# A reordered static schedule for an attention and multiplicative-FFN kernel, meant to issue the loads of the prologue earlier

## The chip, the cores and the metric

The kernel runs on one core of one Trainium2 chip. The metric is the device time of one execution in microseconds (us), best seen as the median of several; the executions of one kernel, six at most in one run, lay within 0.3 to 0.7 % of each other.

The engines are named as in the profile: PE (matmuls), PEld (its weight loads), DVE (vector), ACT (scalar), POOL (GpSimd) and SP, which here mostly issues DMAs.

## The reference, cut to what matters

```python
# 8 batches, 8 heads, 576 positions, 64 wide; float32
q_s = softmax(q, axis=-1);  k_s = softmax(k, axis=2)           # over features, over positions
kv  = einsum('bhsd,bhse->bhde', k_s, v)
x   = einsum('bhsd,bhde->bhse', q_s, kv)  -> (4608, 512)        # tokens x (heads * 64)
a, b = x @ w1, x @ w2                                          # 512 -> 1024, twice
out  = ((a * b) @ w3) @ w_out                                  # 1024 -> 1024 -> 512
```

## The kernel before: the parts that the change and the argument touch

The kernel multiplies W3 by W_out once (`W3O`), runs the attention batch by batch, and feeds groups of tokens to the FFN. Its 1477 steps are made first, as objects; nothing is emitted. Three literal tables then decide everything that a scheduler decides: `ORDER`, the order in which the steps are emitted (and so the order within each engine and each DMA queue, as every engine works in order), `SLOTS`, which buffer of its pool each step's buffer is, and `ENGS`, the engine of each step that can run on more than one.

```python
class Steps:
    ...
    def run(self, order, slots, engs):
        for b, s in zip(self.bufs, slots):
            b.tile = self.pools[b.pool][s]
        for n in order:
            if isinstance(n, tuple):
                self.fill(self.pools[n[0]][n[1]], n[2])      # matmuls on a blank tile
            elif self.tasks[n].alts:
                self.tasks[n].emit(engs[n])
            else:
                self.tasks[n].emit()
...
    tiles("st", 9, [P, 2 * RK * D], F32)      # staging: all loads land here
    tiles("osb", 4, [P, C], F32)              # output rows before their store
    tiles("ps", 8, [P, 512], F32, psum)       # the eight PSUM banks
```

A load takes one of the nine staging buffers. It is issued on the SP queue, behind all loads and SP stores emitted before it, and can't be issued before the step that last read its staging buffer is done. So the order of loads, and the buffers they reuse, decide whether the DMA queue ever runs empty.

```python
    def load(key, nbytes, rate, desc, view, src):
        b = buf("st")
        def emit():
            nc.sync.dma_start(out=view(b.tile), in_=src)
        ld[key] = (add("SP", ("ld",) + key, emit, [], [b], ...), b, view)
```

In the attention of one batch each of q, k and v comes in two pieces (four heads each). For q: exponential on ACT, sum and reciprocal on DVE, then a scaling (`qn`) on DVE or POOL, transposes on PE for batches 0 to 3 and a transposing DMA after, evictions of those (`qv`), and the x matmuls, whose PSUM banks are evicted (`xc`) by DVE or ACT into `xt`. For v: one cast to fp16 (`vc`), on POOL in most cases.

```python
            def norm(e, eq=eq, ds=ds):
                {"POOL": nc.gpsimd, "DVE": nc.vector}[e].tensor_tensor(
                    out=eq.tile, in0=eq.tile, op=ALU.mult, in1=...)   # eq * 1/sum
            ...
            t3 = add("POOL", ("qn", b, i), norm, [tr_], [eq, ds], dict(POOL="nt", DVE="tts"), n=1152)
...
                tx = add("PE", ("x", b, i, r0), xm, tn[i] + t5, [kv2, qsT, xt_buf[g]] + px, ...)
```

The FFN's first group is plain; the later ones use a Strassen-type scheme with seven products, whose sums are taken while PSUM is evicted (names `e1` to `e3`, `k1`, `k2`, `k4`; `k3` and `k5` multiply the two factors of the FFN), with helper sums of x (`tt`), of the weights (`wc`) and, for one group's second product, of `W3O` (`sT`) and of the hidden rows (`sS`). Every PE step needs free PSUM banks, so a late eviction on DVE or ACT stops PE.

The softmax here doesn't subtract the row's maximum and nothing guards it: scores larger than these inputs give would overflow.

## Time and profile before

| | before |
|---|---|
| time, median of 6 runs beside the new kernel | 230.99 us (230.84 to 231.96) |
| span of the profiled run (its time 231.96, the slowest of the six) | 230.0 us |
| span of a second profile of the same kernel (time 230.74) | 228.8 us |
| PE busy | 219.9 us, 96 % |
| DVE, ACT, POOL busy | 182.8, 142.0, 102.2 us |

How to read it: PE is the bound, and all that can be won lies in the few us in which it stands. The busy share doesn't show those well. "Perfetto Trace Analysis" of the Trainium skill says at its head, of a kernel's distance from the roofline, that matmul busy time is a bad metric, because matmuls are pipelined; here too the busy time of PE comes out the same for two kernels 1.5 us apart, as the result shows. So I read the timeline and the chain of waits, and for comparing two orders I use a **lag**: the time at which a PE step starts, minus the work of all PE steps before it (each matmul counted at the distance between starts that the trace shows for its shape). A stretch where the lag stays flat is run at PE's own pace; each rise is a wait.

### The profile page before, as it was taken

The page shows a single profiled execution, that of the slowest core. Times are in us where ns is not written, and L with a number is a line of the kernel's source. Part 1 is how long each engine was busy: PE and PEld are TensorE (multiplying, and loading weights), DVE is VectorE, ACT ScalarE, POOL GpSimd, SP SyncE. Part 2 cuts the span into 40 slices and gives each one's busy share as a digit, 9 for nine tenths or more (in the row PEclk, how much of TensorE's full clock was granted, in tenths as well). Part 3 has the DMA queues.
Part 4 walks back from the last instruction along what each step waited for, and adds up shares of the span by engine and source line. Part 5 has one row for each costly group of instructions (what it writes and reads, how often), then busy time and mean ns, then how long its engine had stood idle before and what let it go on. Part 6 is the DMA issues. An engine that isn't in the chain of part 4 may idle for free.

```text
span 230.0 us, 5284 instructions
## 1 busy us (share of the span) xinstructions
PE 219.9 (96%) x1971; PEld 124.6 (54%) x1971; DVE 182.8 (79%) x392; ACT 142.0 (62%) x289; POOL 102.2 (44%) x84
## 2 busy tenths in 40 slices
PE   7699999999999999999999999999999899999992
PEld 3354548866676564444445656543444367766640
DVE  0332865789999998999967989999999999889820
ACT  2236875768768998777527658766799474354021
POOL 4313745584064990197940268800299920310000
PEclk9999999999999999999999999999999999999999
DMA  6999997981998679919786976669885502124556
GB/s 222 390 404 391 392 388 268 379 330 13 353 371 333 158 242 278 372 50 337 180 211 171 278 278 171 128 111 297 274 204 165 75 0 48 24 68 92 116 131 165
DMA packets 32888, 50.92 MB, mean 221 GB/s; under 512 B 11744, under 2 KB 12000, under 8 KB 32864
## 3 DMA queue, kind: packets, MB, share of 16 engines
q1 hardware_dynamic: 31504, 48.57, 66.5%
q10 hardware_dynamic: 1360, 2.03, 3.8%
q8 instruction: 15, 0.25, 0.5%
q14 instruction: 9, 0.07, 0.1%
HBM read 38.80 MB, written 9.44 MB: 210 GB/s over the span
## 4 chain that ended last, share of the span: by engine, by line
PE 72%; DVE 10%; DMA 8%; ACT 3%; issue 2%; POOL 2%; SPq 2%; DVEq 0%; ACTq 0%
PE ps L648 31%; PE ps L739 17%; PE ps L591 7%; PE ps L377 6%; PE ps L836 5%; DMA st<-in_moe_w_dram 3%; DMA out_dram<-osb 2%; DMA qsT<-eq 2%; DVE cc L672 2%; PE ps L511 2%; PE ps L556 2%; DVE tt L626 2%; DVE ds L459 1%; POOL eq L469 1%; PE ps L485 1%
## 5 line engine op out<-in xcount | busy, mean ns | idle before, releaser
L672 DVE TENSOR_TENSOR cc<-ps,uu 128x512 f16<-128x512 f32 (+3 forms) x120 | 65.2, 570 | 2.8 <-PE ps L648 0.7
L344 ACT COPY uu<-ps 128x512 f32<-128x512 f32 (+3 forms) x107 | 50.4, 501 | 25.9 <-PE ps L648 14.9
L699 POOL TENSOR_TENSOR ab<-cc,cc 128x512 f16<-128x512 f16 (+3 forms) x25 | 23.1, 927 | 70.2 <-DVE cc L672 59.4
L739 PE MATMUL ps<-W3O,ab 128*128 128x512 f16 (+1 forms) x224 | 53.4, 372 | 0.0
L648 PE MATMUL ps<-tt,wc 128*128 128x512 f16 (+3 forms) x240 | 52.1, 334 | 0.3
L648 PEld LDWEIGHTS <-wc 128*128 128x128 f16 x320 | 31.0, 98 | 25.6 <-DVE tt L626 1.4
L648 PE MATMUL ps<-xt,w 128*128 128x512 f16 (+3 forms) x160 | 36.6, 334 | 0.5 <-ACT osb L725 0.5
L648 PEld LDWEIGHTS <-w 128*128 128x128 f16 x240 | 22.6, 98 | 18.1 <-issue 1.8
L739 PEld LDWEIGHTS <-ab 128*128 128x128 f16 x224 | 21.4, 98 | 20.1 <-issue 0.6
L469 POOL TENSOR_TENSOR eq<-eq,ds 128x1152 f16<-128x1152 f16 x13 | 27.9, 2152 | 6.6 <-DVE ds L466 3.3
L725 ACT ACTIVATE osb<-ps 128x512 f32<-128x512 f32 (+1 forms) x24 | 13.3, 566 | 22.5 <-PE ps L739 19.9
L459 DVE TENSOR_REDUCE ds<-eq 128x9 f32<-128x576 f16 x32 | 23.4, 740 | 4.0 <-ACT eq L455 4.0
L672 DVE TENSOR_TENSOR ab<-ps,cc 128x512 f16<-128x512 f32 (+3 forms) x40 | 22.4, 567 | 1.8 <-PE ps L648 0.6
L455 ACT ACTIVATE eq<-st 128x576 f16<-128x576 f32 x32 | 21.5, 686 | 1.1 <-DMA st<-in_q_dram 1.0
L434 ACT ACTIVATE ek<-st 128x576 f16<-128x576 f32 x32 | 21.0, 688 | 1.6 <-DMA st<-in_k_dram 1.3
L344 ACT CAST xt<-ps 128x320 f16<-128x320 f32 (+7 forms) x46 | 15.4, 400 | 9.1 <-PE ps L556 8.9
L648 PE MATMUL ps<-xt,wc 128*128 128x512 f16 (+3 forms) x80 | 20.2, 334 | 0.0
L648 PE MATMUL ps<-tt,w 128*128 128x512 f16 (+3 forms) x80 | 19.7, 334 | 0.0
L591 PE MATMUL ps<-xt,w 128*128 128x320 f16 (+1 forms) x128 | 16.2, 286 | 0.0
L377 PE MATMUL ps<-ab,ab 128*128 128x512 f16 x64 | 14.8, 379 | 0.4 <-ACT ab L344 0.3
L591 PEld LDWEIGHTS <-w 128*128 128x128 f16 x128 | 12.3, 98 | 3.6 <-issue 0.2
L344 POOL CAST v<-st 128x1152 f16<-128x1152 f32 x10 | 12.5, 1261 | 0.8 <-PE ps L511 0.8
(76 smaller groups left out, 251.6 us busy)
## 6 DMA issues: line engine op xcount, KB each, us to landing
st<-in_q_dram SPq DMA_DIRECT2D x16, 576.0 KB, 5.3
st<-in_v_dram SPq DMA_DIRECT2D x16, 576.0 KB, 8.0
st<-in_k_dram SPq DMA_DIRECT2D x16, 576.0 KB, 7.2
st<-in_moe_w_dram SPq DMA_DIRECT2D x16, 512.0 KB, 8.9
out_dram<-osb SPq DMA_DIRECT2D x56, 128.0 KB, 4.1
st<-in_moe_w_out_dram SPq DMA_DIRECT2D x4, 512.0 KB, 7.5
out_dram<-osb ACTq DMA_DIRECT2D x14, 128.0 KB, 2.4
out_dram<-osb ACTq DMA_DIRECT2D x3, 64.0 KB, 2.5
```

What stands on the lines that cost most here:

```text
L344: {"DVE": nc.vector.tensor_copy, "POOL": nc.gpsimd.tensor_copy, "ACT": nc.scalar.copy}[eng](out=o, in_=i)
L377: nc.tensor.matmul(pp.tile, lhsT=wT.tile[:, gt * P:(gt + 1) * P], rhs=wo[i][1].tile[:, (gt % 2) * C:(gt % 2 + 1) * C], start=(gt == 0), st ...
L434: nc.scalar.activation(out=ek.tile[:, :, j, :], func=AF.Exp, in_=vk(bk.tile)[:, j].rearrange("p (r d) -> p r d", r=RK))
L455: nc.scalar.activation(out=eq.tile[:, :, j, :], func=AF.Exp, in_=vq(bq.tile)[:, j].rearrange("p (r d) -> p r d", r=RK))
L459: nc.vector.tensor_reduce(out=ds.tile[:, 0, j], axis=AX.X, op=ALU.add, in_=eq.tile[:, :, j, :])
L469: {"POOL": nc.gpsimd, "DVE": nc.vector}[e].tensor_tensor(out=eq.tile, in0=eq.tile, op=ALU.mult, in1=ds.tile[:, 1].rearrange("p j r -> p r ...
L591: nc.tensor.matmul(ps.tile[:, 0:m], lhsT=w[qt][:, ct, fo:fo + P], rhs=x[:, ct, lo:lo + m], start=(ct == 0), stop=(ct == 3))
L648: nc.tensor.matmul(ps.tile[:, 0:h], lhsT=lhs(c), rhs=rhs(c), start=first and c == 0, stop=c == 1, skip_group_check=not first)
L672: return lambda: nc.vector.tensor_tensor(out=dst(), in0=ps.tile[:, 0:h], in1=other.tile[:, 0:h], op=op)
L699: {"POOL": nc.gpsimd, "DVE": nc.vector}[e].tensor_tensor(out=ab.tile[:, 0:h], in0=c11.tile[:, 0:h], in1=c21.tile[:, 0:h], op=ALU.mult)
L725: nc.scalar.activation(out=o(), in_=i(), func=AF.Copy, scale=ISC)
L739: nc.tensor.matmul(po.tile[:, :w], lhsT=ab_buf[(g, ft)].tile[:, tb * P:(tb + 1) * P], rhs=W3O[:, ft, m * w:(m + 1) * w], start=(ft == 0), ...
```

## The change

Its intent: emit all steps in another order, in which the loads of the prologue are issued ahead of the point where the DMA queue would drain. Only the three tables differ. Nearly all of `ORDER` moves a little, 741 of 874 `SLOTS` and 160 of 447 `ENGS` change; there are 26 fillers instead of 27, DVE has ten more instructions, ACT three more, POOL 13 fewer, and five output stores move from the ACT queue to the SP queue. The first lines of `ORDER` (the rest is cut):

```diff
 ORDER = [
-    ('ps', 7, 9), 6, 12, 4, 14, 1, 10, 3, 2, 96, 0, 97, ('ps', 7, 2), 120, 121, ('ps', 7, 2), 88, 89,
-    ('ps', 7, 3), 90, 128, 98, 5, 129, ('ps', 7, 4), 122, 8, 130, 68, 123, 112, 131, 99, 91, 69, 113, 124,
-    15, 114, 100, 7, 80, 92, 9, 115, 13, 116, 72, 81, 132, 82, 73, 70, 74, 83, 133, 11, 104, 84, 16, 101,
+    ('ps', 3, 12), 6, 2, 14, 10, 12, 1, 3, 96, 4, 80, 0, 81, 128, 97, 8, 129, ('ps', 3, 6), 112, 5, 113,
+    120, 114, 130, 9, 121, ('ps', 3, 2), 7, 68, 122, 15, 82, 115, 131, 69, 83, 98, 123, 132, 88, 84, 124,
+    16, 99, 72, 89, 17, 100, 11, 90, 116, 104, 13, 73, 91, 74, 92, 70, 105, 75, 106, 76, 77, 142, 101, 144,
 ...
```

Steps 0 to 25 are the loads of the prologue: 0 to 8, 10, 12 and 14 are pieces of W3 and W_out, 9, 11, 13, 15, 16, 17 are q, k, v of batch 0, and 18 to 25 are the FFN weights. 26 to 31 are q, k, v of batch 1. The staging buffers of loads 18 to 31, and the engines of the two scalings of batch 0:

```diff
 SLOTS  (staging buffers of loads 18 to 31)
-    8, 0, 7, 4, 6, 2, 3, 5, 0, 6, 1, 4, 7, 8
+    6, 0, 3, 7, 4, 3, 8, 6, 2, 0, 6, 5, 7, 3
 ENGS
-    147: "DVE",  157: "POOL"      # qn of batch 0, first and second piece
+    147: "POOL", 157: "DVE"
```

## The prediction

> **What bounds the kernel now.** I read the page first: busy shares, the forty slices, then the timeline of the tensor engine in the prologue, the load queue's timeline, the table of windows and last the chain that ended last.
>
> ```profile
> PE 219.9 (96%) x1971; PEld 124.6 (54%) x1971; DVE 182.8 (79%) x392; ACT 142.0 (62%) x289; POOL 102.2 (44%) x84
> ...
> PE   7699999999999999999999999999999899999992
> ...
> DMA  6999997981998679919786976669885502124556
> ```
>
> The tensor engine (PE) is busy nearly always; a slice is 5.75 us, so only the first two slices and the last one are loose. The DMA row is full for the first six slices, then has holes. Busy is not useful, so I split the span:
>
> ```profile
> 0.00:11.70 11.70, 8.65 (x52) 3.90 (x53) 2.76 (x5) 3.19 (x3) 4.18 (x13) 1.00 0.83 308
> 11.70:28.30 16.60, 16.28 (x103) 8.40 (x103) 8.49 (x13) 9.81 (x15) 6.95 (x5) 1.00 1.05 396
> 28.30:33.80 5.50, 5.03 (x114) 2.59 (x111) 3.69 (x14) 4.10 (x9) 3.21 (x3) 1.00 1.05 387
> 33.80:225.50 191.70, 189.99 (x1709) 109.73 (x1706) 167.86 (x361) 124.32 (x263) 87.82 (x64) 1.00 0.66 198
> 225.50:230.00 4.50, 0.00 (x0) 0.00 (x0) 0.00 (x0) 0.60 (x1) 0.00 (x0) 1.00 0.61 157
> ```
>
> Columns: stretch and length, then busy time of PE, PEld, DVE, ACT, POOL, then granted clock, DMA share, GB/s. From 11.7 us to 225.5 us PE never rests for long; up to 33.8 the DMA share is full at 387 to 396 GB/s; the last 4.5 us are one eviction and its store. The prologue on PE:
>
> ```profile
> 1.19 3.97 PE L931 MATMUL ps<-blank 128*128 128x512 f16 x9 [1.19 <-DVE blank L924]
> ...
> 11.74 1.89 PE L377 MATMUL ps<-ab,ab 128*128 128x512 f16 x8
> ...
> 29.43 0.82 PE L931 MATMUL ps<-blank 128*128 128x512 f16 x3
> 30.37 0.44 PE L556 MATMUL ps<-qsT,kv 64*64 64x320 f16 x8
> 30.74 1.04 PE L931 MATMUL ps<-blank 128*128 128x512 f16 x4
> 32.09 0.48 PE L511 MATMUL ps<-v,ek 64*64 64x65 f16 x36 [0.32 <-ACT qsT L344]
> 32.60 0.72 PE L591 MATMUL ps<-xt,w 128*128 128x320 f16 x4
> ```
>
> L931 is filler on a blank tile, put where PE has nothing to do; the real work of the FFN starts at 32.60. The load queue:
>
> ```profile
> 19.92 11.26 SPq L310 DMA_DIRECT2D st<-in_moe_w_dram  x8
> 38.62 0.88 SPq L310 DMA_DIRECT2D st<-in_q_dram  x2
> ...
> 42.50 0.37 SPq L310 DMA_DIRECT2D st<-in_v_dram  x1
> 56.10 0.37 SPq L310 DMA_DIRECT2D st<-in_q_dram  x1
> ```
>
> The eighth weight load of the prologue is issued at 30.8 us and lands at 39.9 us; the next load is issued at 38.62 and lands at 42.7. That is the point where the queue drains, some 1.5 us of it.
>
> **What the Trainium skill says.** "TensorE: Matmul & The Clock Gate", section "Wait — 56ns, not 53.3ns?": warm matmuls start N/2.4 GHz + 2.5 ns apart, cold ones N/1.2 GHz. The trace agrees: starts 216 ns apart for 512 columns, 136 for 320, 56 for 128, and 425 ns for the first nine fillers. "DMA: Bandwidth & Descriptors", section "Anatomy of one DMA — SWDGE (gpsimd) path": about 2.0 us fixed per DMA, and waits on semaphores happen at the issuing sequencer before dispatch. These loads go by another path, but a store issued at 220.31 began to land at 222.31, so 2.0 us fits. "GPSIMD Engine Reference", section 3.1: tensor_tensor is about twice as slow on GpSimd as on VectorE. Here it is worse: 2.13 us against 0.68 us for 1024 fp16 elements, 2.15 against 1.40 for the softmax scaling.
>
> **The change, part by part.** Steps, shapes and code are the same; three tables (order, buffer slots, engine of each movable step) differ.
>
> PE work. It is the same but for 26 fillers in place of 27 (-0.2 us, where PE waits anyway). Counts times the starts above, in us: transposes 136 x 56 ns = 7.6, W3·W_out 64 x 216 = 13.8, plain FFN 64 x 110 + 64 x 136 = 15.7, Strassen-type blocks 112 x 122 + 112 x 136 + 112 x 162 + 224 x 216 = 95.4, second product 208 x 216 + 16 x 109 + 112 x 109 = 58.9, and about 13 for the small attention matmuls: 204. So 230 holds 26 us that are not work: 5.2 before the first transpose, 4.5 of tail, about 5 of fillers and waits between 5.2 and 11.7, about 2.3 between 28.3 and 33.8, and the remaining 9 in waits of 0.1 to 0.6 us inside the long stretch and in imperfect overlap of the small matmuls. A gain over 2% (4.6 us) must come out of the last three, 16 us in all.
>
> Prologue loads. The eighteenth load completes q, k, v of batch 0 in both orders, after the same twelve 512 KB and six 576 KB loads; it landed at 29.15 us before. Loads land one every 1.2 to 1.5 us as long as the queue holds work, so it lands there again (estimate). After it: cast on POOL 1.15, kv matmuls 0.48, scale 0.42, x matmuls 0.44, evacuation 0.43, and five hand-overs of about 0.1: first FFN matmul about 32.7 us. The new order has all x matmuls behind it then; the old started the FFN at 32.60 but put two x steps (0.55 us) inside. Gain 0.3 us. Ahead of that, the first W3·W_out product needs w_out's first piece, now sixth in the queue (11.84) instead of fifth (10.52); with 0.69 for its cast it starts at 12.6 rather than 11.74. That eats slack: three transposes instead of four are then left, and 64 x 216 ns still ends near 28 us. No loss.
>
> Drain. The five middle FFN weight loads now wait for the slot of a v piece: lands 26.1, cast to 27.4, so issue at about 27.5, with the queue full to 30.5; 2.0 us of latency leaves 1 us to spare. The next batch's q is issued after a weight cast at about 35.3 instead of 38.62, so it lands near 41.4 instead of 42.7. That closes the 1.5 us hole. What it is worth: batch 1 is first used on PE at 53.8 us, and between 33.9 and 48.3 the chain holds nothing but FFN matmuls. So 0 us. A second hole may open at 43 us behind v of batch 1, whose slot waits for a weight cast queued behind eight products; also hidden.
>
> Engines. DVE gets net ten steps more, POOL 13 fewer. With the trace's means: four weight combinations 4 x 0.68 (from 4 x 2.13 on POOL), two scalings 2 x 1.40, three W3·W_out evictions 3 x 0.65, and smaller moves with signs both ways: DVE +7.0 us of instruction time, with overlap about +6, so near 189 (82%); POOL -18; ACT +3. DVE has 40 us of slack over the span but little of it in stretches: it was busy 93 to 98% from 130 to 190 us. By order, its new load is heavier between 40 and 70 us of PE work (36.3 us of instruction time against 33.3) and at 160 to 170 (14.9 against 13.7). Cost there: I choose 0.5 us.
>
> Later PE order. The landmarks (kv and x of each batch, each transposing DMA) lie within 1.7 us of PE work of their old places. The largest late wait is kept:
>
> ```profile
> 178.75 4.85 DMA qsT<-eq
> 183.64 0.44 PE ps L556 x8
> ```
>
> The last transposing DMA is issued at the same point (159.2 us of PE work) and its reader still stands 3.2 us of work later, less than the 4.85 it took. Tail: same last product, same ACT eviction, two stores: 4.5 us.
>
> Sum: 230 - 0.3 - 0.2 + 0.5 + 0 = 230.0 of profile span; I say 230.3 as the timed median was 1 us above.
>
> **Rivals.** (1) The holes matter more than I think: if earlier loads let the softmax run earlier and DVE and ACT be smoother later, the 9 us of small waits could shrink by 3 to 4: 226 to 227. For: both orders were evidently searched, and waits of 0.6 us at 132 and about 1 us at 183 are there to win. Against: no wait in the long stretch on PE is ended by a load, and the 1 us at 183 stays. (2) DVE becomes the bound: +6 us where it is already full makes PE wait 2 to 4 us more: 232 to 234. For: 93 to 98% busy from 130 us on. Against: half of the added work lies before 130 us, and the weight combinations were put at about 104 and 141 us of PE work, where before DVE had a light stretch (7.5 us in 10). (3) The weight loads issued at 27.5 miss the deadline, the queue drains at 30.5, and the FFN starves: +1 us, 231.3.
>
> **Range and chances.** Prologue +-0.7, long stretch +-2, tail +-0.3: about +-2.2 in all, so 227.8 to 232.8. The 2% lines are 226.4 and 235.6: faster needs rival 1 in full, slower needs 2 and 3 and more.
>
> **What would show it.** Right: DMA full from 1 to about 42 us without the dip at 40; first FFN matmul at 32.7; PE useful stretch within 2 us of 191.7; DVE near 189, POOL near 84; tail 4.5. Wrong: PE waits ended by loads, a DVE row near 99% with PE waits behind it, or the first FFN matmul off by over 1 us.

## The result, and the profile after

| | before | after |
|---|---|---|
| median of 6 runs | 230.99 us | 232.48 us |
| lowest to highest | 230.84 to 231.96 | 232.23 to 233.39 |
| ratio, 95 % interval | | 1.0064 (1.0041 to 1.0087) |

A ratio here and below is the mean time of one kernel's runs over that of the other's of the same rounds, so not quite the ratio of the medians quoted. The new order is **slower by 0.6 %, 1.5 us**: small, but outside the interval. Line numbers of the new kernel are one lower (L648 is L647). Its busy row and slices (a slice is now 5.76 us):

```profile
PE 220.4 (96%) x1970; PEld 125.3 (54%) x1970; DVE 188.1 (82%) x402; ACT 145.2 (63%) x292; POOL 83.9 (36%) x71
...
PE   7799989999999999999999999999999899999992
...
DMA  6999989899982979928576985647966301253355
```

PE's busy time is 220.4 us; the control profile of the old kernel has 220.4 too. DVE and POOL are where the prediction put them. The DMA row no longer has its 7 in the seventh slice (34.5 to 40 us), the hole that the change aimed at; it has an 8 in the sixth and one in the eighth instead. The table of windows (columns as in the prediction) puts a number on the first of these:

```profile
28.30:33.80 5.50, 4.67 (x115) 2.78 (x115) 4.81 (x16) 3.65 (x9) 2.19 (x2) 1.00 0.82 247
33.80:225.50 191.70, 190.12 (x1708) 110.01 (x1707) 171.70 (x369) 125.53 (x264) 73.63 (x54) 1.00 0.65 201
```

Between 28.3 and 33.8 us the DMA share fell from 1.05 (387 GB/s) to 0.82 (247 GB/s). The load queue on SP shows why:

```profile
21.40 14.03 SPq L309 DMA_DIRECT2D st<-in_moe_w_dram  x8
36.81 0.88 SPq L309 DMA_DIRECT2D st<-in_q_dram  x2
42.83 0.37 SPq L309 DMA_DIRECT2D st<-in_v_dram  x1
```

The group of eight weight loads starts at 21.40, but its second is issued only at 28.01 us and lands at 32.68; the first had landed at 30.41. The second q piece of batch 1 is now issued at 36.81 in place of 38.62, yet lands at 43.41 against 42.69, because the last weight before it lands at 41.92 instead of 39.87. The hole at 40 us is closed, one has opened ahead of it (that second weight landed at 31.87 in the old order, so 0.8 us of the queue's time are lost), and one more behind v of batch 1, at 45 us.

The FFN starts later, too. The prologue's end on PE:

```profile
28.24 0.89 PE L484 MATMUL ps<-ident,eq 128*128 128x128 f16 x13 [0.44 <-DVE W3O L343]
...
32.62 0.44 PE L555 MATMUL ps<-qsT,kv 64*64 64x320 f16 x8 [0.20 <-DVE kv L521]
33.46 2.74 PE L590 MATMUL ps<-xt,w 128*128 128x320 f16 x21 [0.40 <-ACT xt L343]
```

The first FFN matmul stands at 33.46 us with all x matmuls behind it. (The old order started at 32.60 with 0.55 us of x matmuls still to do: like for like 33.15.) The chain that ended last explains the stretch. In the control profile of the old kernel it runs through PE itself until 29.15 us, that is, PE has work without a break up to there:

```profile
21.22 6.04 PE ps L377 x28
27.26 0.22 PE ps L485 x4
...
29.63 1.16 ACT ek L434 x2
```

In the new kernel the chain is the load of the second q piece, and after it one step after the other on ACT and DVE:

```profile
12.03 11.11 DMA st<-in_q_dram
...
23.88 1.42 DVE ds L458 x2
25.32 0.28 DVE ds L465
25.62 1.36 DVE eq L468
26.98 1.21 DVE W3O L343 x2
28.24 0.89 PE ps L484 x13
```

The load lands at 23.14 (23.07 in the old order, so it isn't late), then come exponential, sums, reciprocal, scaling, and two evictions of W3·W_out that stand in DVE's queue before PE gets its banks: five us of a chain with no slack in it.

The lag shows where the rest went, in us, from one profile of each kernel:

| PE work done | control of before | after | difference | what lies there |
|---|---|---|---|---|
| 16 | 10.14 | 10.21 | +0.07 | W3·W_out products |
| 22 | 13.21 | 13.83 | +0.62 | first FFN matmuls |
| 40 | 13.26 | 13.83 | +0.57 | end of the plain FFN group |
| 65 | 14.49 | 15.65 | +1.16 | first Strassen-type group |
| 107 | 16.62 | 17.85 | +1.23 | |
| 140 | 18.74 | 19.88 | +1.14 | |
| 150 | 18.75 | 20.53 | +1.78 | clock time 166 to 168 us |
| end | 20.69 | 22.28 | +1.59 | tail 4.5 and 4.6 us |

A third of it is the prologue, a third falls between 40 and 65 us of PE work, and a third near 166 us of clock time; in between, each order wins and loses up to 0.3 us at a time. The other profiles, with those of the experiments below, agree with this when counted in the same way, though not to the last tenth: at 22 us of PE work the four with the old prologue stand at 13.2 to 13.7 and the five with the new one at 13.8 to 14.3; between 40 and 65 us the five with the old order there lose 1.2 us each, those with the new order 1.6 or more; between 145 and 150 us the old order loses nothing in all five, the new one 0.6 or more. I also summed all waits of PE of 0.09 us or more after 33.8 us by the engine whose step ended last before them:

| PE waits ended by | control of before | after |
|---|---|---|
| DVE | 3.09 | 3.91 |
| ACT | 1.33 | 2.16 |
| POOL | 0 | 0.12 |
| PE's own pace (nothing late) | 1.90 | 1.87 |
| a load | 0 | 0 |
| sum | 6.32 | 8.05 |

No single wait is above 0.6 us. The sum grows by 1.7 us where the lag outside the prologue grows by 1.0; the two are counted in different ways (waits below 0.09 us are left out of the sums), and I did not chase the rest.

The loss near 166 us has a load behind it after all, one step removed. On ACT:

```profile
163.39 0.60 ACT L724 ACTIVATE osb<-ps 128x512 f32<-128x512 f32 x1
164.92 0.68 ACT L454 ACTIVATE eq<-st 128x576 f16<-128x576 f32 x1 [0.93 <-DMA st<-in_q_dram]
165.51 0.57 ACT L343 COPY uu<-ps 128x512 f32<-128x512 f32 x1
```

ACT stands 0.93 us for the first q piece of batch 7, which lands at 164.84 us (at 160.51 in the old order), and the eviction behind it in ACT's queue is the one that PE waits 0.38 us for at 166.13. Three output stores stand between that load and the v load ahead of it on the SP queue (the expectation of after_loads says four), and the DMA share is 0.98 to 1.00 from 160 to 170 us.

One more thing stood out: DVE steps of one kind that took twice their usual time. Steps of DVE and POOL in the new kernel, two pairs that overlap and one cast alone:

```profile
25.62 1.36 DVE L468 TENSOR_TENSOR eq<-eq,ds 128x1152 f16<-128x1152 f16 x1
...
161.27 1.59 DVE L789 TENSOR_TENSOR st<-W3O 128x1024 f16<-128x1024 f16 x1
```

```profile
26.27 1.71 POOL L343 CAST v<-st 128x1152 f16<-128x1152 f32 x1 [1.43 <-DMA st<-in_v_dram]
29.20 1.15 POOL L343 CAST v<-st 128x1152 f16<-128x1152 f32 x1 [1.21 <-DMA st<-in_v_dram]
...
160.19 2.13 POOL L625 TENSOR_TENSOR tt<-xt,tt 128x1024 f16<-128x1024 f16 x1 [11.03 <-DVE tt L625]
162.27 1.61 POOL L343 CAST v<-st 128x1152 f16<-128x1152 f32 x1
```

A DVE sum of the second line's shape takes 0.69 us alone; this one takes 1.59, and ends 0.54 us after the POOL step that was under way when it started (162.32). It goes the other way round too: the POOL cast that takes 1.15 us alone takes 1.71 when it starts under DVE's scaling, which ends at 26.98. "SBUF — State Buffer" of the Trainium skill, section "Who interferes with whom", says that DVE and GpSimd share a pair of SBUF ports under an exclusive lock, for DVE steps with two SBUF inputs against GpSimd steps that read SBUF. The trace agrees: the later of the two waits for the other's end, and DVE steps that read PSUM are not stretched (two sums that start at 160.07 beside that POOL step take 1.29 us together, 0.65 each). In the new order three DVE steps with two SBUF operands are held by over 0.3 us (1.30 for 0.68, 0.83 for 0.42, 1.59 for 0.69 us), in the old one a single one (0.73 for 0.42). A held cast on POOL is not new with this order: three v casts are held in it (1.71, 1.51 and 1.61 for 1.15 us), but in the old one the first v cast of all is held for longer. In the control profile:

```profile
26.18 2.27 POOL L344 CAST v<-st 128x1152 f16<-128x1152 f32 x1
```

### The profile page after: what moved, and what is told of

Same layout as the page of the kernel before. It is cut to its first block, busy times and chain, and to the rows that moved or that the text cites. A ratio compares the mean times of both kernels' runs of the same rounds, so it can differ in the third digit from the quotient of the medians. Undisturbed runs are those within 1.5% of the kernel's fastest.

```text
span 230.5 us, 5265 instructions
## 1 busy us (share of the span) xinstructions
PE 220.4 (96%) x1970; PEld 125.3 (54%) x1970; DVE 188.1 (82%) x402; ACT 145.2 (63%) x292; POOL 83.9 (36%) x71
## 3 DMA queue, kind: packets, MB, share of 16 engines
q10 hardware_dynamic: 960, 1.51, 2.5%
## 4 chain that ended last, share of the span: by engine, by line
PE 78%; DMA 8%; DVE 8%; ACT 2%; SPq 1%; issue 1%; DVEq 0%; ACTq 0%
PE ps L647 40%; PE ps L738 20%; PE ps L590 7%; PE ps L835 5%; DMA st<-in_q_dram 5%; DMA st<-in_moe_w_dram 3%; PE ps L555 2%; DVE cc L671 2%; PE ps L484 2%; PE ps L510 2%; SPq L309 1%; PE ps L758 1%; DVE ds L458 1%; DVE kv L521 1%; ACT uu L343 1%
## 5 line engine op out<-in xcount | busy, mean ns | idle before, releaser
L343 ACT COPY uu<-ps 128x512 f32<-128x512 f32 (+3 forms) x112 | 51.8, 504 | 18.3 <-PE ps L647 11.6
L647 PE MATMUL ps<-tt,wc 128*128 128x512 f16 (+3 forms) x240 | 51.3, 334 | 0.3 <-ACT uu L343 0.2
L698 POOL TENSOR_TENSOR ab<-cc,cc 128x512 f16<-128x512 f16 (+3 forms) x22 | 21.2, 968 | 72.2 <-DVE cc L671 72.1
L647 PEld LDWEIGHTS <-wc 128*128 128x128 f16 x320 | 30.8, 98 | 25.6 <-issue 1.4
L647 PE MATMUL ps<-xt,w 128*128 128x512 f16 (+3 forms) x160 | 36.6, 334 | 0.4 <-DVE xt L343 0.4
L647 PEld LDWEIGHTS <-w 128*128 128x128 f16 x240 | 22.4, 98 | 18.0 <-issue 1.4
L724 ACT ACTIVATE osb<-ps 128x512 f32<-128x512 f32 (+1 forms) x26 | 13.8, 549 | 27.4 <-PE ps L738 23.4
L468 POOL TENSOR_TENSOR eq<-eq,ds 128x1152 f16<-128x1152 f16 x11 | 23.6, 2146 | 13.1 <-DVE ds L465 12.1
L647 PE MATMUL ps<-tt,w 128*128 128x512 f16 (+3 forms) x80 | 19.7, 334 | 0.0
L647 PE MATMUL ps<-xt,wc 128*128 128x512 f16 (+3 forms) x80 | 19.4, 334 | 0.0
L343 ACT CAST xt<-ps 128x256 f16<-128x256 f32 (+7 forms) x44 | 15.2, 427 | 5.5 <-PE ps L555 5.4
L343 POOL CAST v<-st 128x1152 f16<-128x1152 f32 x11 | 14.0, 1271 | 7.5 <-DMA st<-in_v_dram 7.5
L590 PE MATMUL ps<-xt,w 128*128 128x256 f16 (+1 forms) x128 | 16.0, 286 | 0.4 <-ACT xt L343 0.4
```

The lines of the kernel that those rows point to most:

```text
L343: {"DVE": nc.vector.tensor_copy, "POOL": nc.gpsimd.tensor_copy, "ACT": nc.scalar.copy}[eng](out=o, in_=i)
L468: {"POOL": nc.gpsimd, "DVE": nc.vector}[e].tensor_tensor(out=eq.tile, in0=eq.tile, op=ALU.mult, in1=ds.tile[:, 1].rearrange("p j r -> p r ...
L590: nc.tensor.matmul(ps.tile[:, 0:m], lhsT=w[qt][:, ct, fo:fo + P], rhs=x[:, ct, lo:lo + m], start=(ct == 0), stop=(ct == 3))
L647: nc.tensor.matmul(ps.tile[:, 0:h], lhsT=lhs(c), rhs=rhs(c), start=first and c == 0, stop=c == 1, skip_group_check=not first)
L698: {"POOL": nc.gpsimd, "DVE": nc.vector}[e].tensor_tensor(out=ab.tile[:, 0:h], in0=c11.tile[:, 0:h], in1=c21.tile[:, 0:h], op=ALU.mult)
L724: nc.scalar.activation(out=o(), in_=i(), func=AF.Copy, scale=ISC)
```

## The experiments

The theory to test: **closing the drain is worth nothing, because nothing on PE's path waits for what lands there; the 1.5 us come from a redrawn set of small waits on evictions.** The rivals: (a) the earlier loads do bring something, which a bad prologue eats; (b) the prologue is the whole loss; (c) DVE's extra work is the cause; (d) the buffers, PSUM banks or staging, are the cause, not the order; (e) the one late load near 166 us, or the held DVE steps, are the cause. All kernels gave correct results; each was timed in five rounds against the old kernel on the same chip. The columns: median, ratio to the old kernel, span of the profiled run.

| run | median us | ratio (95 %) | span |
|---|---|---|---|
| before_again | 231.08 | 0.9999 (0.9977 to 1.0021) | 228.8 |
| before_early | 231.18 | 0.9985 (0.9959 to 1.0011) | 229.2 |
| before_psum | 230.92 | 0.9971 (0.9947 to 0.9996) | 228.8 |
| head_after | 231.62 | 1.0016 (1.0000 to 1.0032) | 230.1 |
| head_before | 232.63 | 1.0059 (1.0042 to 1.0077) | 231.3 |
| after_slots | 232.58 | 1.0048 (1.0028 to 1.0068) | 231.1 |
| after_psum | 232.66 | 1.0047 (1.0020 to 1.0075) | 231.1 |
| after_pool | 236.35 | 1.0204 (1.0173 to 1.0234) | 234.9 |
| after_swap | 233.44 | 1.0090 (1.0067 to 1.0112) | 231.0 |
| after_st | 235.45 | 1.0185 (1.0159 to 1.0212) | 233.5 |
| after_both | 235.38 | 1.0177 (1.0149 to 1.0205) | 233.2 |
| after_loads | 233.34 | 1.0093 (1.0063 to 1.0123) | 231.5 |

The old kernel's medians beside them were 231.38 (before_again, the two heads, after_slots), 231.64 (before_early, the two psum runs, after_pool) and 231.25 to 231.29 (the rest); each of these groups ran on one chip. The edits are shown as edits of the tables.

### before_again: the old kernel as a control

```diff
 (no edit)
```

> A control: the old kernel unchanged. One of its six times was 231.96 us and that one is the profiled one; the other five were 230.84 to 231.01. Theory A (two timing modes, about 1 us apart, in every kernel): ratio 1.000 within 0.2%, with some single runs about 1 us high, and a new profile whose span is 229.0 us rather than 230.0 if it falls in the short mode. Rival: the 1 us is the cost of profiling, then every profiled run shows it.

Measured: 0.9999. The rival falls too: this profiled run was the fastest of its six. What follows: the method holds to about 0.2 %, and one profile of a kernel may stand 1 us from another (230.0 and 228.8 here).

### before_early: the old order, with only the change's idea

The old order is kept whole; two staging buffers are exchanged from the second q piece of batch 1 on, so that this load waits for a buffer that comes free earlier.

```diff
 SLOTS  (staging buffers)
-    q_1_1: 6,  v_1_1: 8,  (five later buffers: 6, 6, 6, 8, 6)
+    q_1_1: 8,  v_1_1: 6,  (five later buffers: 8, 8, 8, 6, 8)
```

> The idea of the change alone, in the old kernel: two staging slots swapped for all loads from batch 1 on, so that the first load of batch 1 takes a slot that is free at 32.6 us instead of one free at 38.6 us and goes out before the queue drains at 40 us. Order and engines are the old ones. Theory A (no PE wait after 33 us is ended by a load, so the hole is free): ratio 0.998 to 1.002, with the loads of batch 1 landing 1 to 1.5 us earlier and no hole at 40 us. Rival (the hole costs its 1.5 to 2 us): ratio 0.992 to 0.994.

The load queue of this run:

```profile
32.33 4.68 SPq L307 DMA_DIRECT2D st<-in_q_dram  x2
37.06 0.46 SPq L307 DMA_DIRECT2D st<-in_k_dram  x1
37.61 1.13 SPq L307 DMA_DIRECT2D st<-in_v_dram  x2
```

The second q piece is issued early enough, and lands at 41.71 instead of 42.36; the second k piece lands 2 us sooner (49.16 for 51.14), and the hole at 40 us is gone. The time is that of the old kernel (0.9985, the interval holds 1), and up to 65 us of PE work the lag stays a constant 0.13 us above the control's, within 0.01 us. What follows: the closed hole is worth **nothing**. That is the theory, and it ends rival (a) for this hole. (The expected 1 to 1.5 us of earlier landing were 0.65 for this piece.)

### head_after and head_before: the prologue apart from the rest

```diff
 head_after:   ORDER, SLOTS, ENGS of the new kernel up to 21 us of PE work, of the old one from there,
               with five SLOTS reassigned at the seam
 head_before:  the other way round, with seven SLOTS reassigned at the seam
```

> The mirror image: the new prologue up to 21 us of PE work, then the old order. Theory A: ratio to the old 1.001 to 1.002. Theory B: ratio 1.006, the whole loss.

> The new kernel with the old prologue: all steps up to 21 us of PE work in the old order, with the old slots and engines, the rest in the new order. Theory A (the loss of 1.5 us sits mostly after the prologue, at the batch boundaries where DVE carries more): it gains only 0.2 to 0.5 us on the new kernel, ratio to the old 1.004 to 1.006. Theory B (the loss is the new prologue with its later weight loads and later x steps): it runs as the old kernel, ratio 0.999 to 1.001.

head_after costs 0.16 % (0.24 us by the medians, interval down to 1.0000). Its profile shows a lag 1.3 us above the control's by 30 us of PE work and no more than that to the end, but that profile fell on one of its two slowest runs. head_before doesn't give a clean answer: its prologue is at 13.73 us of lag at 22 us of PE work, and the next 8 us lose another 1.1 us at the seam, in two waits of 0.53 and 0.59 us for evictions on DVE; that PSUM banks and fp16 buffers of the two orders don't fit each other there is my reading, not shown. What follows: the new prologue costs something, less than the whole (rival (b) is not enough). The seam is a miss that teaches: an order and its buffers are one thing, and a half of one doesn't fit to a half of another.

### after_slots, before_psum and after_psum: are the buffers the cause?

In after_slots the staging buffers are rotated for the loads from the second middle FFN weight on, so that this load doesn't wait for the v cast. In the psum runs each PSUM tile gets the bank that by the times of the trace came free first; the order is kept.

```diff
 after_slots  SLOTS, staging, 31 entries:  3 -> 7, 7 -> 0, 0 -> 8, 8 -> 4, 4 -> 3
 before_psum  SLOTS, PSUM banks, 260 entries, and the banks of the fillers
 after_psum   SLOTS, PSUM banks, 259 entries, and the banks of the fillers
```

> The new kernel, with the staging slots of all loads from the second middle FFN weight load on renamed by one rotation, so that these loads take slots that are free by 24 us and no longer wait for the cast of a v piece. Closes the hole in the load queue at 29 to 31 us. If that hole costs time (theory B in its narrow form): 0.7 to 1.5 us faster than the new kernel, ratio to the old 1.000 to 1.003. If loads are hidden at that point (theory A): within 0.2% of the new kernel, ratio 1.005 to 1.007, with the middle weight loads landing 1 to 1.5 us earlier.

> The old kernel, each PSUM tile given the bank whose last reader ended earliest in the measured trace instead of the one in its slot table; order and engines are the old ones. Theory A' (the waits of PE behind PSUM banks still being read by DVE or ACT are part of the 6.3 us of waits in the long stretch): 0.5 to 1.2 us faster, ratio 0.995 to 0.998. Rival (the same waits come back at the data dependency just behind): 0.999 to 1.001.

> The same for the new kernel. Theory A': its waits behind banks are larger (0.6 us before the first transpose of q at 28.2 us, more at 58, 126 and 158 us), so it gains 0.8 to 1.5 us, ratio to the old 0.9995 to 1.003. Rival: 1.005 to 1.007, unchanged.

after_slots: 1.0048, against 1.0064 of the new kernel: the intervals overlap. The hole at 29 us is closed (the second weight load lands at 32.21, 1.37 us after the first), another opens at 39 us, and its lag at 22 and 40 us of PE work is 14.15, no better; near 166 us it loses 0.95 us (the new kernel 0.64). after_psum: 1.0047; its prologue is better (13.45 at 22 us of PE work), but 0.77 us comes back at 42 us of PE work and 1.5 us near 150. before_psum: 0.9971, the best ratio, so perhaps 0.7 us better than the old kernel; its interval is just clear of 1, one of twelve, so this is **not shown**. What follows: buffers are worth some tenths of a us at most. With PSUM banks given by one and the same rule, the two orders still stand 1.7 us apart (232.66 and 230.92, side by side), so rival (d) falls for the banks; for the staging buffers it falls where this one rotation goes.

### after_pool: less work on DVE

```diff
 ENGS
-    217: "DVE", 580: "DVE", 670: "DVE", 685: "DVE"          # scaling of batch 1, three k5 of the first such group
-    1182: "DVE", 1183: "DVE", 1184: "DVE", 1185: "DVE"      # the four sT
+    217: "POOL", 580: "POOL", 670: "POOL", 685: "POOL"
+    1182: "POOL", 1183: "POOL", 1184: "POOL", 1185: "POOL"
```

> The new kernel with eight steps put back from DVE to POOL: the four combinations of the second weight, three products of group 1 and one softmax scaling, some 5 us of DVE time. Theory C (the extra DVE load is what lengthened the waits): 0.5 to 1.0 us faster than the new kernel, ratio to the old 1.002 to 1.004. Rival (it is the order in which DVE and ACT serve PE, not how much they carry): within 0.3 us of the new kernel, 1.005 to 1.007.

Measured: 1.0204, worse than the new kernel by 3.2 us by the ratios (3.9 by the medians), not better. Up to 95 us of PE work its lag is that of the new kernel within 0.35 us, though four steps, 2.3 us of DVE time alone, left DVE around 40 to 60 us of PE work. But DVE got hardly any freer: the scaling moved to POOL at 52.05 us held DVE's other scaling, which took 1.36 us in the new kernel:

```profile
52.83 2.58 DVE L464 TENSOR_TENSOR eq<-eq,ds 128x1152 f16<-128x1152 f16 x1
```

From 45 to 75 us DVE is busy 28.16 us, against 28.46 in the new kernel. So the run does not test rival (c) in that stretch, and the rival stays open. Then it loses 3.7 us more than the new kernel between 100 and 107 us of PE work:

```profile
120.69 3.27 DVE L464 TENSOR_TENSOR eq<-eq,ds 128x1152 f16<-128x1152 f16 x1
```

```profile
118.37 2.12 POOL L785 TENSOR_TENSOR st<-W3O 128x1024 f16<-128x1024 f16 x1
120.57 5.38 POOL L785 TENSOR_TENSOR st<-W3O,st 128x1024 f16<-128x1024 f16 x2
```

```profile
125.21 0.80 PE L506 MATMUL ps<-v,ek 64*64 64x65 f16 x70 [2.12 <-DVE osb L722]
```

The DVE scaling, 1.37 us alone, is held to 3.27 us by the POOL sums that were moved, the evictions behind it in DVE's queue come late, and PE stands 2.12 us at a stretch. What follows: here, moving work off a busy DVE onto an idle POOL cost more than it freed where the two met.

### after_swap: mending the prologue

The two head halves of batch 0 exchange places in loads and steps, three FFN products are hoisted ahead of the last x matmuls, and the last filler goes.

```diff
 ORDER  (all loads and steps of batch 0 trade places with their twins; the loads)
-    9 ... 15 ... 16 ... 17 ... 11 ... 13        # q, q', k', v', k, v of batch 0
+    15 ... 9 ... 11 ... 13 ... 16 ... 17
 ENGS
-    147: "POOL", 157: "DVE"
+    147: "DVE",  157: "POOL"       # and four evictions; 30 SLOTS follow
```

> The new kernel with the two halves of batch 0 exchanged in the prologue (every load and step of half 0 takes the place of the same step of half 1) and three FFN products, which need half 0 alone, moved from behind the last x step to ahead of it, in place of three fillers. Theory D (the prologue's loss is that the new order puts all four x steps ahead of the first FFN product, so that the last chain of kv, scale, x and eviction, some 1.7 us, is bare): lag of PE after the prologue 0.8 to 1.3 us smaller than the new kernel's 13.8 us, ratio to the old 1.001 to 1.003. Rival (the start is set by the last load and its cast alone): no change, 1.005 to 1.007.

Measured: 1.0090, if anything worse than the new kernel. At 20 us of PE work it is 1.05 us ahead of the new kernel, one product later it has lost it:

```profile
31.96 1.06 PE L586 MATMUL ps<-xt,w 128*128 128x320 f16 x6 [0.53 <-DVE xt L339]
...
33.97 0.71 PE L586 MATMUL ps<-xt,w 128*128 128x256 f16 x4 [0.58 <-DVE xt L339]
34.91 3.28 PE L586 MATMUL ps<-xt,w 128*128 128x256 f16 x25 [0.22 <-DVE w L339]
```

The FFN begins 1.5 us earlier (31.96 for 33.46), then waits for evictions of x on DVE twice, and for a weight cast on DVE. What follows: the prologue's wait is not one wait but a row of them on the same engine; starting PE earlier brings it sooner to the next.

### after_st and after_both: the late wait near 166 us by way of the sT sums

The four sums `sT` go to POOL, at the places they had in the old order, to clear DVE near 160 us. after_both adds the edit of after_swap.

```diff
 ENGS
-    1182: "DVE", 1183: "DVE", 1184: "DVE", 1185: "DVE"
+    1182: "POOL", 1183: "POOL", 1184: "POOL", 1185: "POOL"
 ORDER  (1182, 1183, 1184 move up by some 80 to 360 places, 1185 down by some 100; three SLOTS)
```

> The new kernel with the four combinations of the second weight moved to POOL and to the places in the order that they have in the old kernel, clear of any DVE step that reads two SBUF operands; nothing else. Theory E (the 0.65 us lost at 165 us is DVE held by one of these combinations, 1.6 us instead of 0.7, as POOL's own two-operand step ran at the same time): that loss goes, and the 1 us around 124 us shrinks; 0.6 to 0.9 us faster than the new kernel, ratio to the old 1.0025 to 1.0045. Rival (the wait at 165 us comes from the order of ACT's evictions): within 0.2 us, 1.0055 to 1.007.

> Both mends together. If D and E hold and add up: 1.4 to 2.2 us faster than the new kernel, ratio to the old 0.997 to 1.0005, that is as fast as the old one or a little faster. If one fails: 1.001 to 1.005.

Measured: 1.0185 and 1.0177. The wait near 166 us stays, 0.79 us long, as ACT still stands 1.34 us for the late q load; so `sT` on DVE was not its cause, or not the only one (the load itself landed 0.4 us later against the work of PE). A loss of 1.7 us, 0.2 in the new kernel, stands near 90 to 95 us of PE work, at 113 us of clock time: there the multiplication `k5` of one product takes 1.96 us on DVE instead of 0.42, held by the POOL sum that runs from 109.54 to 111.67:

```profile
109.98 1.96 DVE L695 TENSOR_TENSOR ab<-cc,cc 128x512 f16<-128x512 f16 x1
```

```profile
109.54 2.13 POOL L786 TENSOR_TENSOR st<-W3O 128x1024 f16<-128x1024 f16 x1 [0.86 <-ACT ek L430]
```

after_both is no better than after_st alone: the edit of after_swap brings nothing. What follows: rival (e) falls in the shape "the held sums cost the late wait", and the hold itself is confirmed a second time at another place.

### after_loads: the late load itself, and one of the held steps

```diff
 ORDER
-    ... (three stores) ... 62 ...        # 62: load of the first q piece of batch 7
+    62 ... (three stores) ...
-    242 ... (first POOL k5)              # 242: cast of v of batch 2 on POOL
+    (first POOL k5) ... 242
```

> The new kernel with two steps moved in the order, nothing else: the load of q of the last batch goes directly behind a v load, ahead of four stores and 2 us earlier in the queue; and the POOL cast of v of batch 2 goes behind POOL's first product of group 1, so that it no longer runs while DVE does a combination of two SBUF operands at 56 us. Theory F: (1) ACT stands 0.9 us at 164 us waiting for that q load, with an eviction that PE needs queued behind it; the load then lands near 163 us, ACT does not wait, and the 0.65 us that PE loses there (145 to 150 us of PE work) falls to 0.2 or less. (2) DVE is held 0.6 us at 56 us by the POOL cast; without it, PE's loss between 42 and 46 us of PE work falls from 1.3 to about 0.8 us. Together 0.8 to 1.1 us off the new kernel, ratio to the old 1.0015 to 1.003. Rival G (waits taken away at one point come back at the next, as in the exchange of halves): ratio 1.005 to 1.007, with the loss shown a few us later.

Measured: 1.0093, no better than the new kernel. The load lands at 163.60 instead of 164.84, as wanted; but the stores that it passed come later, and ACT now stands for an output buffer:

```profile
165.43 0.60 ACT L720 ACTIVATE osb<-ps 128x512 f32<-128x512 f32 x1 [2.00 <-DMA out_dram<-osb]
```

PE waits 0.82 and 0.62 us at 166 to 167 us, and the loss there grows from 0.65 to 1.70 us. The other half of the edit worked in the small: the weight sum that was held for 1.30 us takes 0.68 again, and that stretch of PE work loses 1.09 instead of 1.29 us. What follows: near 166 us the DMA queue is full, so a load and the stores compete for it, and putting this load first only chose which of two waits PE got. One held step is worth 0.2 us here.

## Why the prediction was right or wrong

The range (227.8 to 232.8) held the 232.48, 0.3 us inside its upper end, and the change stayed within 2 %. That is owed to the width of the range: the prediction saw no change, and the new order is slower by 1.5 us, clear of the noise. The point value was 2.2 us too low: 0.7 us of it in the base (its terms for the change sum to 0, so it put the old kernel at 230.3, against 230.99 measured), 1.5 us in the change. Step by step:

- **The drain is worth 0 us.** Right, and shown: before_early closes the hole alone and gains nothing. The place of the gain was right as well: PE works on FFN matmuls alone there.
- **"issue at about 27.5 ... leaves 1 us to spare".** Wrong by two terms. The v cast was put at 1.15 us, with its end at 27.4; it took 1.71 us and ended at 27.98, since DVE's scaling held it. (The profile that it started from had such a cast: the first v cast takes 2.27 us there.) The issue followed at 28.01, still 0.5 us early by the prediction's count of 2.0 us up to 30.5. But 30.5 is a landing, and the rate of the transfers had fallen 2 us before it: 339 GB/s from 28.0 to 28.5 us, 107 in the next half us. The load landed at 32.68, 4.67 us after its issue, and the queue lost 0.8 us: rival 3 in its first half. Its second half, that the FFN starves, did not come: PE waited for x at 33.46, not for a weight. Hence q of batch 1 landed at 43.41 and not near 41.4. Still hidden.
- **"five hand-overs of about 0.1: first FFN matmul about 32.7".** Wrong by 0.8 us. The sum took each step of the chain at its own duration. The scaling had been moved to DVE, ahead of evictions that PE needed, and the four steps that end the chain stood in DVE's and ACT's queues. A gain of 0.3 us (0.45 by its own 33.15 and 32.7) was a loss of 0.3, like for like, and 0.6 by the lag. That term was in the prediction's own table of engines (a scaling to DVE) but not in its chain.
- **Base of the sum, 230.** The profile it started from was the slowest of its kernel's runs. The control stands at 228.8, and times are 1.9 us above spans, which makes 230.7. "The timed median was 1 us above" compared the span of one run with the time of others; the 0.3 us added for it was too little.
- **Cost of the denser DVE: "I choose 0.5 us".** The small waits in the long stretch grew by 1.7 us, half of it on DVE (+0.8) and half on ACT (+0.8), or by 1.0 us by the lag. The direction of rival 2 was right; whether its cause was, stays open, since after_pool did not free DVE at 40 to 60 us of PE work. Its place was not right: in the old order DVE was busy 88 to 98 % from 130 to 190 us, not 93 to 98, and in the new order less than before there (55.5 for 57.3 us). ACT's half, with a late load behind a part of it, was not in the prediction; it had looked for loads that end a PE wait directly, and there are none.
- **DVE near 189, POOL near 84, tail 4.5, ACT +3.** 188.1, 83.9, 4.6 and +3.2.

What stays open: no mend brought the new order back to the old one's time. The three places of loss (prologue about 0.6, 40 to 65 us of PE work about 0.6, near 166 us about 0.6) are sized from one profile of each kernel (those of the other runs show the same places, with sizes a few tenths apart), and every attempt to remove one of them gained nothing clear of the noise or met another wait soon after. That the loss is the sum of such waits fits all runs; what causes each, and that each has just the size given, is not shown, and whether less work on DVE would mend it (rival (c)) is not tested.

## What to carry to other kernels

A hole in the DMA queue is worth only what an engine on the path waits for behind it: find the first reader of the late transfer, and if it stands many us later, filling the hole can gain nothing, as here. In this static order, which keeps its bound engine 96 % busy, a wait that was removed was mostly given back at the next eviction or buffer, so estimate from the queue of the evicting engine, not from the durations of a chain. Take two profiles of the kernel before, and before you move work from DVE to an idle POOL, look at which DVE steps with two SBUF operands it will run beside.

## What the Trainium skill lacked or had wrong

- "SBUF — State Buffer", section "Who interferes with whom": the exclusive lock between DVE and GpSimd is as it says, but its only sizes are two ratios that name no operation (a DVE one 6.8 times slower, a GpSimd one 1.5 times). Here a held DVE step took 1.59 for 0.69, 1.96 for 0.42 and 3.27 for 1.37 us, and a held POOL cast 1.71 and 2.27 for 1.15 us; the step waits for the other's end and then takes nearly its usual time. What it costs PE ranged from 0.2 us (one held weight sum) to 2.12 us at a stretch (a scaling with evictions behind it).
- "GPSIMD Engine Reference", section 3.1: the factor of about two between GpSimd and VectorE, measured there in fp32, is too low for this kernel's fp16 sums: 2.13 against 0.69 us for 1024 elements a partition, a factor of 3.1; its scaling of fp16 rows by fp32 reciprocals had 2.15 against 1.37 us, a factor of 1.6.
- No page that I read says what an idle stretch of a load queue is worth: here closing one of 1.5 us gained nothing (ratio 0.9985, interval 0.9959 to 1.0011).
- No page that I read says how far two profiles of the same kernel may stand apart: here 230.0 and 228.8 us of span.
